# A two-layer convolution and feed-forward kernel: the even and odd tiles, the filter tiles and the squares of its start in another order

## The chip, the cores and the metric

The kernel runs on one core of a Trainium2 chip. Its time is the device time of one launch in microseconds (us). The kernel before the change took 943.13 us (median of three runs, 942.17 to 943.75).

Five engines of the core work side by side, each through its own list of instructions in order: TensorE (PE, matrix products; its weight loads are shown as PEld), VectorE (DVE), ScalarE (ACT), GpSimd (POOL) and SyncE (SP). PE writes to PSUM, from where DVE or ACT have to take ("evacuate") the result before the buffer can be written again. SP, POOL and ACT also issue the DMA transfers.

## The reference

Two kinds of layers alternate over a sequence of S = 2048 tokens with D = 576 channels, each twice: a gated long convolution A and a gated feed-forward B.

```python
def A(q, k, v, shift_k, ssm_k, ssm_D):
    kv = short_conv(k, shift_k) * v            # 4 taps per channel
    y  = irfft(rfft(kv, 2S) * rfft(ssm_k, 2S))[:S] + kv * ssm_D
    return q * y
def B(x):
    return (gelu(x @ w_gate) * (x @ w_up)) @ w_down     # 576 -> 4608 -> 576
x = A_q
x = x + A(layernorm(x)); x = x + B(layernorm(x))
x = x + A(layernorm(x)); x = x + B(layernorm(x))
```

The convolution y doesn't depend on x, so both A layers use the same y; only the gate q differs.

## The kernel before

**Tiling.** The sequence is cut into 4 blocks of 512 tokens (NB = 4, BS = 512). The convolution is a block convolution in the frequency domain: each block of kv and of the filter h is taken to 512 frequencies with a matrix product by a cosine and a sine matrix, the spectra are multiplied and summed over pairs of blocks, and an inverse product gives y of a block. A tile of frequencies (kt = 0 to 3) has 128 frequencies on the partitions and two parts s (cosine and sine) of 576 channels in the free dimension, which is cut in halves h of 288 (HW), one PSUM bank each. Filter tiles are made by `fwd_h` (line 182; 8 matmuls per part), kv tiles of block 0 by `fwd_full` (191; 8 matmuls per part). The matrices G (for h), F1 and F2 (for kv and the inverse) are made on the chip: angles, a mask on DVE (`mask`, 121), a sine on ACT (`sines`, 124).

Tokens lie four to a partition (i = 0 to 3). The frequencies of tile kt + 2 differ from those of tile kt by the sign of the odd i alone. `fwd_full` makes tiles 2 and 3 with a negated copy (`neg`) of the odd tokens. For the other blocks, `fwd_eo` (202) makes the sum of the even and that of the odd tokens in the two halves of a PSUM tile, 4 matmuls for each part and half of the channels; ACT copies both to an `eo` tile in float32, and `cross` (214) adds and subtracts them on DVE, which gives the tiles kt and kt + 2.

**Stages.** `Conv.begin` (476) writes the start of the kernel in a fixed order, engine by engine as the lines stand: matrices, kv of block 0, the filter tiles of all four blocks, y of block 0 (`inv0`), and then for each of the four 128-token groups j of block 0 a gate (`gate0`: two operations on DVE, then the mean on POOL, line 834, and the sum of squares on ACT, 842), its root on POOL (`root0`: 849, 850), the normalization on DVE (`norm0`, 1017), nine transposes on PE (`turn0`, 1028) and two copies on DVE (`copy0`, 1036). When all four groups are copied to xnT, the feed-forward matmuls (gu, line 1116) can begin. From there on a planner with a simple model of the engines' times (`Pace`) puts the convolution of the later blocks between the feed-forward matmuls. The change is in `begin` alone; the planner's order is the same after it.

**Buffers in the start.** `Conv.ps` (111) hands out PSUM tiles by turns, three from the pool that the transposes use too (3 buffers) and one from a pool with one buffer. Filter tiles of blocks 0, 2 and 3 go to buffers of the pools c_hr and c_kr and are stored to DRAM (Hd); those of block 1 stay in H1 and are stored too. Stores are not issued at once: `spill` (265) puts them in a list, and `flush` (271) issues what is in it on POOL; `h_tile` (571) and `kfwd` (612) flush what stood there before they add their own. The transposed filter blocks are loaded by `load_h` (493) on SP in two buffers, so that block 3's load waits until block 1's tiles have been made. Loads of weights (wgu, wd) are issued on SP too, k, v and x on POOL.

Of the kernel before, what the change touches and what calls it, by code (L numbers as in the profile page):

```python
# [14 lines left out]
BF16 = mybir.dt.bfloat16  # L15
# [3 lines left out]
P = 128  # L19
# [4 lines left out]
HW = 288  # L24
# [32 lines left out]
class Conv:  # L57
# [418 lines left out]
    def begin(self, gate0, root0, norm0, turn0, copy0, x0_stats, more, scratch, wide, stay):  # L476

        tc, nc, D = self.tc, self.nc, self.D
        with ExitStack() as es:
# [4 lines left out]
            ones = tmp.tile([1, P], BF16, name="ones")  # L484
# [8 lines left out]
            def load_h(b):  # L493
                t = hp.tile([P, RT, D], BF16, tag="h", name="h")
                nc.sync.dma_start_transpose(out=t[:], in_=self.hk[:, b * BS:(b + 1) * BS])
                return t
# [22 lines left out]
            G = tmp.tile([P, RT, 2 * NFQ], BF16, name="G")  # L519
# [2 lines left out]
            neg = scratch(BF16)  # L522
            jg = [ang[:, g * 4 * 2 * P:(g + 1) * 4 * 2 * P] for g in range(2)]
            jg.append(None)
            ps = self.ps()
            for _ in range(32):
                nc.tensor.matmul(ps[:, 0, 0:16], lhsT=ones[:], rhs=ones[:, 0:16], start=True, stop=True)

            def taps(j):
                ps = self.ps()  # L530
                for h in range(2):
                    nc.tensor.matmul(ps[:, h, 0:HW], lhsT=ones[:], rhs=sk1[:, h * HW:(h + 1) * HW, j], start=True, stop=True)
                nc.scalar.copy(out=self.halves(self.skc[:, j, :]), in_=ps[:, :, 0:HW])
# [8 lines left out]
                    taps(2)  # L542
            taps(1)
            taps(0)
            hT = {0: hp.tile([P, RT, D], BF16, tag="h", name="h")}
            for g in (1, 0):
                pt = self.psp.tile([P, 2, 1024], BF16, tag="pr", name="hps")
# [10 lines left out]
            flat = lambda F: F.rearrange("p i s j q -> p (i s j q)")  # L558

            def f_angles(g):  # L560
                if g == 2:
                    jg[2] = tmp.tile([P, 2, NFQ], I32, tag="dft_j", bufs=2, name="dft_j")[:].rearrange("p s f -> p (s f)")
                j4 = jg[g].rearrange("p (i s f) -> p i s f", i=2, s=2)
                cv = (colf[:] if g == 2 else col[:, 0:2, :]).rearrange("p t q -> p (t q)")
                for i in range(2):
                    row = 2 * i if g == 2 else 2 * g + i
                    for s in range(2):
                        nc.scalar.activation(out=j4[:, i, s, :], in_=cv, func=ACT.Identity, bias=offs[:, s:s + 1],
                                             scale=rowf[:, row:row + 1])

            def h_tile(b, kt, pool):
                if b == 1:
                    t = self.H1[:, kt, :, :]
                else:
                    t = pool.tile([P, 2, D], BF16, tag="kr" if pool is self.krp else "hr", name="h0")
                for s in range(2):
                    self.fwd_h(G, hT[b], kt, s, t)
                self.flush(0.0)
                self.spill(self.Hd[b][kt], t)
                return t  # L580
            h0 = {}
            self.H1 = stay()
            kv0 = deque(self.kv_ops(0))
# [3 lines left out]
            def negate(n):  # L587
                nc.scalar.mul(out=neg[:, n, :], in_=self.vt_[0][:, 2 * n + 1, :], mul=-1.0)
            for i in range(RT):
                h0[KTS[i]] = h_tile(0, KTS[i], self.hrp if i == 0 else self.krp)  # L590
                for _ in range(4):
                    kv0.popleft()[1]()
                if i == 1:
                    negate(0)
                if i < 2:
                    self.mask(jg[i])
                    self.sines(flat(Fs[i]), jg[i])
                if i < 1:
                    f_angles(i + 1)
                if i == 1:  # L600
                    more(0)
            hT[2] = load_h(2)
            h_tile(1, 0, self.hrp)
            more(1)
            h_tile(1, 2, self.hrp)
            self.load_k(1, nc.gpsimd)
            x0_stats(0)
            x0_stats(1)
            negate(1)
            kc, A = {}, {}  # L610

            def kfwd(kt):
                kc[kt] = self.kcp.tile([P, 2, D], BF16, tag="kc", name="kc")
                for s in range(2):
                    self.fwd_full(self.vt_[0], neg, kt, s, kc[kt])
                self.flush(0.0)
                self.spill(self.Kd[0][kt], kc[kt])

            def kacc(kt):
                for part in range(2):  # L620
                    t = self.ybp.tile([P, D], BF16, tag="yb", name="yb")
                    self.prod(part, kc[kt], h0[kt], t[:])
                    A[(part, kt)] = t
# [3 lines left out]
            def pair0(kt, sg):  # L627
                for part in range(2):
                    b = self.ybp.tile([P, D], BF16, tag="yb", name="yb")
                    nc.vector.tensor_tensor(out=b[:], in0=A[(part, kt)][:], in1=A[(part, kt + 2)][:],  # L630
                                            op=ALU.subtract if sg else ALU.add)
                    self.yb[(part, kt, sg)] = b

            def inv0(mt):
                self.inverse(0, mt, [(self.lhs(kt, s, mt, self.F2), self.yb[(s, kt, mt % 2)])
                                     for kt in range(2) for s in range(2)])
            kfwd(0)
            f_angles(2)
            kfwd(2)
            kacc(0)  # L640
            self.mask(jg[2])
            kfwd(1)
            kacc(2)
            self.sines(flat(self.F2[:]), jg[2])
            pair0(0, 0)
            kfwd(3)
            kacc(1)
            self.load_v(1, nc.gpsimd)
            kacc(3)
            pair0(1, 0)  # L650
            nc.scalar.activation(out=warm[:], in_=self.pis[:, 1:2], func=ACT.Gelu_apprx_tanh)
            h_tile(1, 1, self.hrp)
            h_tile(1, 3, self.hrp)
            hT[3] = load_h(3)
            h_tile(2, 0, self.hrp)
            h_tile(2, 2, self.krp)
            inv0(0)
# [9 lines left out]
            def kv1_ops(n):  # L667
                for _ in range(n):
                    next(ops)[1]()
            gate0(0)  # L670
            gate0(2)
            root0(0)
            gate0(1)
            h_tile(2, 1, self.hrp)
            root0(2)
            norm0(0)
            h_tile(2, 3, self.krp)
            gate0(3)
            root0(1)
            turn0(0)  # L680
            norm0(2)
            copy0(0)
            root0(3)
            norm0(1)
            h_tile(3, 0, self.hrp)
            turn0(2)
            copy0(2)
            norm0(3)
            turn0(1)
            copy0(1)  # L690
            turn0(3)
            kv1_ops(2)
            copy0(3)
            h_tile(3, 2, self.krp)
            kv1_ops(6)
            h_tile(3, 1, self.hrp)
            h_tile(3, 3, self.krp)
# [523 lines left out]
```

## Time and profile before

| | |
|---|---|
| time, median of three runs | 943.13 us |
| the profiled execution's own time | 943.32 us |
| its span | 941.5 us |
| PE busy | 926.9 us (98%) |
| DVE busy | 571.4 us (61%) |
| ACT busy | 295.9 us (31%) |
| POOL busy | 143.2 us (15%) |
| gu matmuls (L1116) | 565.5 us |
| first gu matmul, from the span's start | 62.71 us |

The busy times are sums over the whole span; a PE that is busy is not a PE at its peak. The profile's page gives the busy share in 40 slices of 23.5 us each, the first three of which hold the part of the kernel that the change touches. The chain of waits follows the work that ended last back from the last instruction, at each step to what released it. In the list of instructions in order of time, a line gives the start, the duration from the first start to the last end of the merged instructions, the engine, the line of the kernel, the operation, what is written from what, and how many instructions are merged; in brackets stands the idle time of the engine before it and what ended that. The lines of 2 us stretches give start and end, their length, then busy us (and instructions) of PE, PEld, DVE, ACT and POOL, the granted clock of PE, the busy share of the DMA engines and GB/s.

### The profile page before, as it was taken

Reading aid. Unit: us, or ns where it says so; the run is one execution under the profiler, and the core shown is the slowest. Engines: PE = TensorE matmul, PEld = TensorE weight load, DVE = VectorE, ACT = ScalarE, POOL = GpSimd, SP = SyncE. Lnnn points to the kernel's source line nnn. Section 1 sums busy time; section 2 is a strip of 40 time slices with the busy share of each in tenths; the row PEclk is TensorE's granted clock in tenths of the full one; section 3 lists DMA queues with packets and bytes.
Section 4 is the critical chain, followed back from the end, with each engine's and each line's share of the span. In section 5 each row is a group of like instructions: output and inputs, shape, how many; then the busy total and the mean of one; then the engine's idle time right before and its main releaser. Section 6 shows DMA issues by size and latency. Waiting matters only on the chain.

```text
span 941.5 us, 19061 instructions
## 1 busy us (share of the span) xinstructions
PE 926.9 (98%) x8128; PEld 536.5 (57%) x8128; DVE 571.4 (61%) x1027; ACT 295.9 (31%) x541; POOL 143.2 (15%) x303
## 2 busy tenths in 40 slices
PE   7989999999999999999999999999999999999998
PEld 5755564665655646546546556556556556556555
DVE  8977887898898637988982333663333335523332
ACT  8846214432124334231222421441221223311211
POOL 2453100511123104230100100230000002100000
PEclk9999999999999999999999999999999999999999
DMA  7989986765953522983930630891630630797720
GB/s 184 323 238 274 293 183 148 133 162 142 226 190 64 113 77 52 195 212 87 221 107 2 133 94 26 136 156 39 129 99 1 129 98 14 135 206 155 147 65 26
DMA packets 129065, 127.46 MB, mean 135 GB/s; under 512 B 45587, under 2 KB 121684, under 8 KB 128980
## 3 DMA queue, kind: packets, MB, share of 16 engines
q1 hardware_dynamic: 119904, 90.85, 45.7%
q0 software_dynamic: 8944, 34.49, 11.4%
q8 instruction: 63, 1.03, 0.5%
q10 hardware_dynamic: 132, 0.91, 0.4%
q14 instruction: 22, 0.18, 0.1%
HBM read 105.58 MB, written 10.62 MB: 123 GB/s over the span
## 4 chain that ended last, share of the span: by engine, by line
PE 91%; DMA 3%; DVE 2%; POOL 2%; ACT 1%; issue 1%; SPq 0%; POOLq 0%; DVEq 0%
PE gu L1116 59%; PE dn L1132 27%; DMA h<-in_A_ssm_k_dram 2%; PE cps L208 1%; PE cps L261 1%; PE ps L187 1%; DMA k<-in_A_k_dram 1%; POOL rstd L850 1%; PE ps L198 1%; DVE x_c L1161 0%; PE cps L187 0%; POOL ve L849 0%; ACT junk L842 0%; DVE x_c L877 0%; DMA xnT<-xn 0%
## 5 line engine op out<-in xcount | busy, mean ns | idle before, releaser
L1116 PE MATMUL gu<-xnT,wgu 64*128 64x512 bf16 x5184 | 565.5, 376 | 2.1 <-DVE x_c L1161 1.0
L1116 PEld LDWEIGHTS <-wgu 64*128 64x128 bf16 x5184 | 254.3, 94 | 305.2 <-issue 10.1
L1120 ACT ACTIVATE ga<-gu 128x512 f32<-128x512 f32 x288 | 171.9, 597 | 549.9 <-PE gu L1116 541.1
L1121 DVE TENSOR_TENSOR hT<-ga,gu 128x512 bf16<-128x512 f32 x288 | 197.6, 686 | 221.2 <-ACT ga L1120 219.7
L1132 PE MATMUL dn<-wd,hT 128*128 128x288 bf16 x2304 | 291.0, 286 | 0.5 <-DVE ob L1141 0.5
L1132 PEld LDWEIGHTS <-hT 128*128 128x128 bf16 x2304 | 223.5, 98 | 66.1 <-issue 10.5
L1166 DVE TENSOR_TENSOR x_c<-x_c,dn 128x576 f32<-128x576 f32 x64 | 48.2, 753 | 82.3 <-PE dn L1132 82.0
L834 POOL TENSOR_SCALAR nm<-s 128x1 f32<-128x1 f32 x60 | 21.1, 352 | 344.1 <-DVE x_c L1161 215.1
L842 ACT ACTIVATE junk<-x_c,nm 128x576 bf16<-128x576 f32 x48 | 37.0, 771 | 40.8 <-POOL nm L834 40.8
L327 POOL DMA_DIRECT2D hr<-Hd x32 | 17.3, 541 | 161.2 <-DVE prod L228 161.2
L850 POOL TENSOR_TENSOR rstd<-ve,neghalf_t 128x1 f32<-128x1 f32 x60 | 39.9, 665 | 5.0
L229 DVE TENSOR_TENSOR sum<-prod 128x576 bf16<-128x576 bf16 x72 | 33.0, 458 | 2.5
L187 PEld LDWEIGHTS <-G 128*128 128x128 bf16 x256 | 25.5, 100 | 11.2 <-issue 2.2
L187 PE MATMUL ps<-h,G 128*128 128x288 bf16 x192 | 27.6, 298 | 2.5 <-DMA h<-in_A_ssm_k_dram 1.7
L1152 DVE TENSOR_TENSOR ob<-x_c,dn 128x576 bf16<-128x576 f32 x15 | 11.2, 753 | 27.2 <-PE dn L1132 19.0
L163 DVE TENSOR_TENSOR kvt<-k,skc 128x1152 bf16<-128x1152 bf16 x32 | 23.9, 754 | 0.5
L849 POOL TENSOR_SCALAR ve<-ss 128x1 f32<-128x1 f32 x60 | 18.1, 301 | 32.4 <-ACT junk L842 32.3
L216 DVE TENSOR_TENSOR kc<-eo 128x288 bf16<-128x288 f32 x48 | 19.2, 453 | 2.1 <-ACT eo L211 2.1
L877 DVE SCALAR_TENSOR_TENSOR x_c<-g_t,rstd,x_c 128x576 f32<-128x576 f32 x16 | 13.1, 818 | 12.0 <-POOL rstd L850 11.9
L211 ACT COPY eo<-cps 128x576 f32<-128x576 f32 x24 | 15.3, 636 | 15.2 <-PE cps L208 12.7
L269 POOL DMA_DIRECT2D out_dram<-ob x12 | 6.7, 555 | 86.3 <-DVE ob L1152 86.2
L383 DVE TENSOR_TENSOR zs<-sum 128x576 f32<-128x576 bf16 x24 | 18.1, 755 | 0.5
(112 smaller groups left out, 464.7 us busy)
## 6 DMA issues: line engine op xcount, KB each, us to landing
wgu<-in_B_w_gate_dram SPq DMA_DIRECT2D x45, 576.0 KB, 5.7
wd<-in_B_w_down_dram SPq DMA_DIRECT2D x30, 864.0 KB, 6.7
wgu<-in_B_w_up_dram SPq DMA_DIRECT2D x45, 512.0 KB, 8.2
hr<-Hd POOLq DMA_DIRECT2D x32, 288.0 KB, 5.3
kr<-Kd POOLq DMA_DIRECT2D x24, 288.0 KB, 5.4
Hd<-h POOLq DMA_DIRECT2D x12, 288.0 KB, 4.6
Kd<-kc POOLq DMA_DIRECT2D x12, 288.0 KB, 6.6
k<-in_A_k_dram POOLq DMA_DIRECT2D x3, 1008.0 KB, 6.1
```

The source lines that it names most:

```text
L163: nc.vector.tensor_tensor(out=st[dst][:], in0=self.kt_[b][:, s0:s0 + 2, :], in1=self.skc[:, j, :].unsqueeze(1).to_broadcast([P, 2, D]), op ...
L187: nc.tensor.matmul(ps[:, h, 0:HW], lhsT=G[:, i, s * NFQ + kt * P: s * NFQ + (kt + 1) * P], rhs=src[:, i, h * HW:(h + 1) * HW], start=(n == ...
L216: self.nc.vector.tensor_tensor(out=dst, in0=eo[:, 0, :], in1=eo[:, 1, :], op=op)
L229: nc.vector.tensor_tensor(out=dst, in0=pr[:, 0, :], in1=pr[:, 1, :], op=ALU.subtract if part == 0 else ALU.add)
L834: nc.gpsimd.tensor_scalar(out=v["nm"][:], in0=v["s"][:], scalar1=-1.0 / D, scalar2=None, op0=ALU.mult)
L842: nc.scalar.activation(out=junk[:], in_=get_x(), func=ACT.Square, bias=v["nm"][:, 0:1], accum_out=v["ss"][:])
L850: nc.gpsimd.tensor_tensor(out=v["rstd"][:], in0=ve[:], in1=neghalf_t[:, 0:1], op=ALU.pow)
L1116: nc.tensor.matmul(pair[:, s, :], lhsT=w[r0:r0 + HK, k, gi * P:(gi + 1) * P], rhs=xnT[r0:r0 + HK, b, :], start=(k == 0), stop=(k == NKC - 1))
L1120: nc.scalar.activation(out=ga[:], in_=pair[:, 0, :], func=ACT.Gelu_apprx_tanh)
L1121: nc.vector.tensor_tensor(out=hT[:, fi, :], in0=ga[:], in1=pair[:, 1, :], op=ALU.mult)
L1132: nc.tensor.matmul(acc[:, h, 0:HW], lhsT=hT[:, fi, j * P:(j + 1) * P], rhs=wd[2 * wb + fi // WT][:, fi % WT, h * HW:(h + 1) * HW], start=( ...
L1166: nc.vector.tensor_tensor(out=xh, in0=xh, in1=acc[:, :, 0:HW], op=ALU.add)
```

## The change

Five things are changed in `begin`:

1. The tiles 0 and 2 of kv of block 0 are made by `fwd_eo` and `cross` as for the later blocks, in place of two calls of `kfwd` (two of `fwd_full` each). The statistics of x (`x0_stats`) stand after the matmuls, and their second half between the crosses.
2. The tiles (1,1) and (1,3) of the filter stand between the kv tiles 0/2, 1 and 3, and the load of the filter's block 3 behind (1,3). They stood behind all kv tiles.
3. The sines of F2 are issued behind the last kv tile's evacuations, and no longer ahead of them.
4. Filter tiles can be made in halves (one part s at a time, `h_half`). The tiles (2,1), (2,3), (3,0) and (3,2) are put in halves between the gates, roots, norms and transposes of block 0, so that the squares on ACT stand by turns with the evacuations of these halves.
5. Sixteen more of the small matmuls on `ones` (the kernel begins with 32 of them) stand ahead of the transposes of the first filter block.

```diff
+            warm_up(32)
...
             taps(0)
+            warm_up(16)
...
+            def h_half(b, kt, pool):
+                s = 1 if (b, kt) in half else 0
+                if s == 0:
+                    half[(b, kt)] = self.H1[:, kt, :, :] if b == 1 else pool.tile(
+                        [P, 2, D], BF16, tag="kr" if pool is self.krp else "hr", name="h0")
+                t = half[(b, kt)]
+                self.fwd_h(G, hT[b], kt, s, t)
+                if s == 1:
+                    self.flush(0.0)
+                    self.spill(self.Hd[b][kt], t)
+                return t
             def h_tile(b, kt, pool):
...
+                h_half(b, kt, pool)
+                return h_half(b, kt, pool)
...
             self.load_k(1, nc.gpsimd)
-            x0_stats(0)
-            x0_stats(1)
             negate(1)
...
-            kfwd(0)
+            for kt in (0, 2):
+                kc[kt] = self.kcp.tile([P, 2, D], BF16, tag="kc", name="kc")
+            eos = []
+            def eo0(s, h):
+                eos.append((s, slice(h * HW, (h + 1) * HW), self.fwd_eo(self.vt_[0], 0, s, h)))
+            def cross0():
+                s, cols, eo = eos.pop(0)
+                self.cross(eo, kc[0][:, s, cols], kc[2][:, s, cols])
+            for s in range(2):
+                for h in range(2):
+                    eo0(s, h)
+            x0_stats(0)
             f_angles(2)
-            kfwd(2)
+            for n in range(4):
+                cross0()
+                if n == 1:
+                    x0_stats(1)
+            self.flush(0.0)
+            for kt in (0, 2):
+                self.spill(self.Kd[0][kt], kc[kt])
             kacc(0)
+            h_tile(1, 1, self.hrp)
             self.mask(jg[2])
             kfwd(1)
             kacc(2)
-            self.sines(flat(self.F2[:]), jg[2])
+            h_tile(1, 3, self.hrp)
+            hT[3] = load_h(3)
             pair0(0, 0)
             kfwd(3)
+            self.sines(flat(self.F2[:]), jg[2])
             kacc(1)
...
             nc.scalar.activation(out=warm[:], in_=self.pis[:, 1:2], func=ACT.Gelu_apprx_tanh)
-            h_tile(1, 1, self.hrp)
-            h_tile(1, 3, self.hrp)
-            hT[3] = load_h(3)
             h_tile(2, 0, self.hrp)
...
             gate0(0)
+            h_half(2, 1, self.hrp)
             gate0(2)
+            h_half(2, 1, self.hrp)
             root0(0)
+            h_half(2, 3, self.krp)
             gate0(1)
-            h_tile(2, 1, self.hrp)
             root0(2)
             norm0(0)
-            h_tile(2, 3, self.krp)
+            h_half(2, 3, self.krp)
+            turn0(0)
+            h_half(3, 0, self.hrp)
             gate0(3)
             root0(1)
-            turn0(0)
             norm0(2)
             copy0(0)
             root0(3)
             norm0(1)
-            h_tile(3, 0, self.hrp)
+            h_half(3, 0, self.hrp)
             turn0(2)
             copy0(2)
             norm0(3)
+            h_half(3, 2, self.krp)
             turn0(1)
             copy0(1)
+            h_half(3, 2, self.krp)
             turn0(3)
             kv1_ops(2)
             copy0(3)
-            h_tile(3, 2, self.krp)
             kv1_ops(6)
```

## The prediction

> **What bounds the kernel now.** I read the page's 40 slices first (TensorE, PE, is full from the fourth slice on), then the chain of waits, then the first 63 us engine by engine, since every edit lies there: the first big matmul (gu, L1116) starts at 62.71 us. After it PE has no idle time up to 150 us, and 2.1 us in the 780 us from there on. So the change is worth what it moves that start, microsecond for microsecond.
>
> The chain of waits for these 63 us:
>
> ```profile
> 2.31 8.77 DMA k<-in_A_k_dram
> ...
> 21.18 2.12 PE ps L187 x16
> ...
> 37.05 15.08 DMA h<-in_A_ssm_k_dram
> ...
> 62.77 15.65 PE gu L1116 x144
> ```
>
> It names PE from 21 us and then the load of filter block 3. But a chain shows one of several tight paths. The busy time in stretches of 2 us (PE, PE's weight loads, VectorE = DVE, ScalarE = ACT, GpSimd = POOL) shows a second one:
>
> ```profile
> 26.00:28.00 2.00, 2.00 (x18) 1.61 (x17) 1.90 (x7) 1.79 (x4) 1.12 (x2) 1.00 0.96 249
> ...
> 36.00:38.00 2.00, 2.00 (x18) 1.52 (x16) 1.93 (x5) 1.99 (x6) 0.26 (x1) 1.00 1.05 408
> ...
> 42.00:44.00 2.00, 2.00 (x19) 1.60 (x17) 1.88 (x4) 1.30 (x2) 0.00 (x0) 1.00 1.09 341
> ```
>
> PE and DVE are both full: DVE's missing 0.03 to 0.12 us are the steps between instructions, and the view of waits names none for it from 24.65 to 48.2 us. The instructions in order of time show where they meet:
>
> ```profile
> 40.44 2.29 DVE L630 TENSOR_TENSOR yb<-yb 128x576 bf16<-128x576 bf16 x6
> 42.74 0.82 DVE L801 SCALAR_TENSOR_TENSOR x_c<-x_b,mv,y 128x576 f32<-128x576 bf16 x1
> ...
> 40.88 2.12 PE L261 MATMUL ps<-yb,F 128*128 128x288 bf16 x16
> ...
> 49.86 0.66 PE L1028 MATMUL xps<-ident,xn 128*128 128x128 bf16 x9 [0.98 <-ACT h L189]
> 52.17 2.13 PE L187 MATMUL ps<-h,G 128*128 128x288 bf16 x16 [1.65 <-DMA h<-in_A_ssm_k_dram]
> ...
> 56.22 0.68 PE L1028 MATMUL xps<-ident,xn 128*128 128x128 bf16 x9 [0.90 <-DVE xn L1017]
> ...
> 62.71 15.71 PE L1116 MATMUL gu<-xnT,wgu 64*128 64x512 bf16 x144
> ```
>
> PE enters the inverse (L261) at 40.88, just as DVE makes its inputs (L630); DVE enters the first gate (L801) at 42.74, just as the inverse is evacuated (42.06 + 0.65). After that PE has 3.5 us of holes, in brackets.
>
> **The change part by part.** Durations come from this execution; a 288-column matmul counts at its pitch, 0.98 us / 8 = 0.1225 us.
>
> The even and odd tiles. Two kfwd calls (2 x 2 x 8 = 32 matmuls) become four fwd_eo calls of 4: 16 fewer, 16 x 0.1225 = 1.96 us off PE. ACT still makes four evacuations (0.64 us each, L200 before, L211 later in this trace). DVE gains eight crosses: six of L216 later in the trace take 2.32 us, pitch (2.32 - 0.45) / 5 = 0.373, so 8 x 0.373 = 2.98 us, and nothing is taken off DVE. Their inputs come in time: the first eo copy ends near 27.05 (H1's last evacuation at 25.30, negate, copy, at 0.53 to 0.58 a step), DVE comes to it at 24.65 + 2 x 1.22 of statistics = 27.09. From 24.65 on DVE waited for nothing, so all that follows moves by 2.98: the second group of pair sums from 40.44 to 43.42, the first gate from 42.74 to 45.72.
>
> PE after the edit: four eo groups end at 25.10 + 1.96 = 27.06; tiles (1,1), kv 1, (1,3), kv 3, (2,0), (2,2) take 6 x 1.96 = 11.76, and 0.3 is lost where (1,3) waits for a PSUM buffer, because the four f_angles on ACT (2.07 us) now stand ahead of (1,1)'s evacuations: 39.2. Two of the four terms of inv0(0) take 0.49: 39.7. The third needs pair0(1,0), 43.42 + 0.45 = 43.9. PE stands still for 4.2 us: more than it was spared. The other 28 matmuls of the inverse, 3.43, with 0.25 for the fourth term, end at 47.5; (2,1) and (2,3) 3.92 later, at 51.45. Each evacuation of the inverse is done at least 0.3 us before its gate, so the gates keep DVE's time.
>
> Gates and the first transpose. Gates 0, 2 and 1 take 1.665 each (42.74, 44.41, 46.07): DVE is through at 50.7. norm0(0) needs POOL, whose order the edit alters: the store of tile (2,2), which stood behind rstd of gate 0, now stands ahead of it, since half tile (2,1) flushes it.
>
> ```profile
> 46.24 0.72 POOL L834 TENSOR_SCALAR nm<-s 128x1 f32<-128x1 f32 x1 [0.93 <-DVE x_c L806]
> 46.92 0.18 POOL L849 TENSOR_SCALAR ve<-ss 128x1 f32<-128x1 f32 x1
> 47.19 0.98 POOL L850 TENSOR_TENSOR rstd<-ve,neghalf_t 128x1 f32<-128x1 f32 x1
> ...
> 51.98 0.20 POOL L849 TENSOR_SCALAR ve<-ss 128x1 f32<-128x1 f32 x1
> 52.26 0.57 POOL L850 TENSOR_TENSOR rstd<-ve,neghalf_t 128x1 f32<-128x1 f32 x1
> ```
>
> ve would start at 46.92 + 2.98 + 0.54 to 0.62 (the issue) = 50.5; ve and rstd took 1.29 to the norm at 46.92, 0.88 at 51.98, so norm0(0) starts at 51.4 to 51.8, ends 0.70 later, and turn0(0) starts at 52.1 to 52.5. Before, it started at 49.86, held 0.98 by an evacuation queued behind three squares; the squares by turns remove that hold, but the transpose is later by more.
>
> The tail. From turn0(0) to gu the after kernel has four turns (0.52 each), and tiles (3,0) to (3,3) (1.96 each): 9.9 us. DVE's copies free the PSUM buffers of the halves of (3,2) about 0.2 us late, twice; with semaphores 0.5 in all. gu: 62.5 to 62.95. Before, the same work took 62.71 - 49.86 = 12.85: it held the 1.65 for block 3's filter and the 0.90, and a late turn now comes when PE has less left behind it, because half tiles stand between the gates.
>
> Moves at no cost. load_h(3) waits on SP for the last read of (1,3), 33.3 instead of 36.9; if it takes 15.1 as before it lands at 48.5, and its first reader comes at 52.6; cover 4 us, beyond that one for one. The third wgu load behind it on SP goes with it. load_v(1) on POOL waits for kv 3 to leave PE, 35.3 instead of 33.25; it lands some 9 us later, is read by L173 (63.04 before). The statistics' second half comes 1.5 us later and is used at 45.7. The last sines move on ACT from 32.64 to about 36, with the table load (1.28) behind them, so (2,0)'s evacuation ends at 39.05; inv0(0)'s buffer waits for that, and is covered by the wait for DVE. Halving the tiles adds no instruction. The 16 warm-up matmuls (32 took 1.02, so 0.5) stand at 5.6, where PE next waits for hn until 7.39; without that cover the 0.5 would reach DVE's copy at 9.78, and 0.05 of it the start of kv at 11.10, which waits for k.
>
> Sum on the profiled run's own time (943.32, span 941.5 plus 1.8; median shown 943.13): gu -0.2 to +0.25, so 943.1 to 943.6; I take the middle, **943.3**. On this kernel 0.2% (1.9 us, like the scatter 942.17 to 943.75) is what can be told from no change.
>
> **A rule against it.** PE's matmuls have two rates here, though the granted clock says 1.00 throughout:
>
> ```profile
> L187 PE MATMUL ps<-h,G x13: 396/444/448, 9.7 to 12.9; 128*128 128x288 bf16 x13
> ...
> L187 PE MATMUL cps<-h,G x7: 286/286/286, 13.7 to 14.5; 128*128 128x288 bf16 x7
> ```
>
> 444 ns while PE had just begun, 286 after some 6 us of work (7.39 to 13.3). From 48.9 to 52.2 PE did only 0.5 us of transposes and stayed at 286; a hole of 4.2 us is not in this trace. The Trainium skill, TensorE: Matmul & The Clock Gate, part 1, says that after an idle window of about 3.4 us the clock is halved, and that windows run freely; by it, as my estimate, such a hole would cool PE in about (4.2 - 3.4) / 3.4, a quarter, of the runs, with the sum of the second rival (945.0), and not otherwise. No stretch here shows which.
>
> **The rivals.**
> 1. PE is the bound after all, as the chain has it. Then 1.96 and the holes 0.98, 1.65 and 0.90 go: 5.5 us, 937.8. For it: PE is full from 21 to 48.9. Against: DVE's floor. Even with POOL at no time, norm0(0) ends at 50.7 + 0.7 = 51.4, and gu cannot start before 61.4 (942.0).
> 2. The hole of 4.2 us halves PE's rate (slower). Place: inverse and tile (2,1), from 43.9. At the 5.9 us that the start took to recover, half of it, 2.95, is lost: turn0(0) at 54.4, PE-bound from there, gu at 54.4 + 9.9 + 0.1 = 64.4, **945.0**; at 3.4 us cold 0.7, and with inverse tiles also late for gates 2 and 1 (0.4 to 0.6 each) up to 3: 944 to 946.5. It decides once PE's slack before turn0(0), 0.65 to 1.05, is used up. For: the 444 ns rows; against: the stretch from 48.9.
> 3. Block 3's filter, fetched while all DMA queues are full (share 1.0 to 1.3 from 38 to 50), lands after 52.6, or another wait in the tail: 945 to 946, only if the load takes over 19 us.
>
> **How the numbers follow.** Forecast 0.50; rival 1 0.12; rival 2 0.28, a good half beyond +0.2%; rival 3 and what I do not see 0.10. Faster 0.12; slower 0.16 + 0.10 = 0.26; same 0.50 + 0.12 = 0.62. The range leaves out rival 1 and the top of the others: 942.0, DVE's floor, to 946.0.
>
> **What would show it.** Right: pair0's group of six near 43.4, the first gate near 45.7, PE idle some 4 us inside inv0(0), turn0(0) near 52.3, no wait for block 3's filter, gu within 0.5 us of 62.7. Rival 2: matmuls of 444 ns behind the hole. Wrong: an inverse that does not wait for DVE, or DVE idle between 27 and 45 us.

## The result, and the profile after

The kernel after the change takes 945.01 us (median of 8 executions, 943.69 to 946.39) against 942.87 for the kernel before beside it (8 executions, 941.48 to 943.75): ratio 1.0025, 95% interval 1.0015 to 1.0036. Measured again unaltered in a later session (12 executions, below) it took 943.72 against 942.80: 1.0014, 1.0003 to 1.0026. So by the medians the change costs 0.9 to 2.1 us. That is at the edge of the 0.2% that was taken as the bound of what can be told; both intervals lie above 1. The forecast, 943.3, was 1.7 us under the first median and 0.4 under the second. The second rival, a hole that halves PE's rate, had 945.0.

The profiled execution of after took 944.92 us (span 943.2); its first big matmul starts at 64.58 us instead of 62.71. Own time less that start is 880.3 us, before 880.6; over the two kernels and all experiments it lies between 879.8 and 880.8. So all that follows is about the first 65 us.

The chain of waits of after between 9 and 66 us (start, us, engine, what, instructions):

```profile
26.79 0.65 ACT H L189
27.44 0.57 ACT ang L600
28.02 0.54 ACT eo L211
28.58 1.56 DVE kc L216 x4
...
45.07 0.38 DVE yb L640
45.49 0.77 PE ps L261 x4
46.27 1.57 PE cps L261 x8
47.83 3.04 PE ps L261 x16
...
54.80 0.50 PE xps L1061 x9
...
64.65 1.40 PE gu L1149 x11
```

Before, the chain ran over PE and then hung on block 3's filter load. Now it enters DVE with the first cross (L216) at 28.58, stays on DVE for 17 us, and goes to PE with the inverse (L261) at 45.49; from there PE has no more idle time up to gu. The filter load is gone from it.

The same in the instructions in order of time, DVE and then PE (idle time before, and what ended it, in brackets):

```profile
25.20 0.81 DVE L819 BATCH_NORM_STATS2 stats<-x_b 128x6 f32<-128x288 bf16 x2
...
28.58 1.56 DVE L216 TENSOR_TENSOR kc<-eo 128x288 bf16<-128x288 f32 x4 [0.85 <-ACT eo L211]
...
44.99 2.29 DVE L640 TENSOR_TENSOR yb<-yb 128x576 bf16<-128x576 bf16 x6
47.20 0.81 DVE L834 SCALAR_TENSOR_TENSOR x_c<-x_b,mv,y 128x576 f32<-128x576 bf16 x1
...
45.49 0.77 PE L261 MATMUL ps<-yb,F 128*128 128x288 bf16 x4 [4.24 <-DVE yb L640]
46.10 1.73 PE L261 MATMUL cps<-yb,F 128*128 128x288 bf16 x8
47.63 3.25 PE L261 MATMUL ps<-yb,F 128*128 128x288 bf16 x16
...
54.63 0.67 PE L1061 MATMUL xps<-ident,xn 128*128 128x128 bf16 x9
...
64.58 1.69 PE L1149 MATMUL gu<-xnT,wgu 64*128 64x512 bf16 x14
```

The second group of pair sums (L640, x6) moved from 40.44 to 44.99, the first gate (L834) from 42.74 to 47.20. PE stands still for 4.24 us inside the inverse. The 28 matmuls behind that hole take from 45.49 to 50.71, 5.2 us; at the pitch of 0.1225 they would take 3.43. The stretches of 2 us (after the length: PE, PEld, DVE, ACT, POOL, then the granted clock) say why:

```profile
42.00:44.00 2.00, 0.00 (x0) 0.00 (x0) 1.93 (x5) 0.18 (x1) 0.23 (x1) 1.00 1.03 406
...
46.00:48.00 2.00, 2.00 (x12) 1.37 (x11) 2.00 (x5) 0.78 (x2) 0.00 (x0) 0.63 1.03 362
48.00:50.00 2.00, 2.00 (x11) 1.26 (x10) 1.79 (x5) 0.73 (x2) 0.73 (x1) 0.52 1.14 234
50.00:52.00 2.00, 2.00 (x18) 1.60 (x17) 1.97 (x4) 1.53 (x3) 1.25 (x2) 1.00 1.19 237
```

From 42 to 44 us PE does nothing while DVE is full. From 46 to 50 the clock is granted at 0.63 and 0.52, and PE, busy all the time, starts 12 and 11 matmuls in a stretch that holds 18 in a warm one.

This execution has a second such place, earlier, which the next execution of the same kernel did not have:

```profile
19.05 4.77 PE L187 MATMUL ps<-h,G 128*128 128x288 bf16 x24 [2.01 <-ACT h L189]
```

PE stood for 2.01 us, the clock fell to 0.50 between 20 and 22, and 24 matmuls took 4.6 us instead of 2.94. PE thus reached the even and odd sums at 26.59 (before, kv's first tile at 25.10), and DVE had to wait 0.85 for the first copy, the bracket at 28.58.

### The profile page after: what moved, and what is told of

It is laid out like the page before. It is cut to its first block, busy times and chain, and to the rows that moved or that the text cites. A ratio compares the mean times of both kernels' runs of the same rounds, so it can differ in the third digit from the quotient of the medians.

```text
span 943.2 us, 19070 instructions
## 1 busy us (share of the span) xinstructions
PE 928.3 (98%) x8128; PEld 536.4 (57%) x8128; DVE 574.4 (61%) x1035; ACT 295.5 (31%) x541; POOL 140.6 (15%) x303
## 4 chain that ended last, share of the span: by engine, by line
PE 91%; DVE 4%; POOL 1%; DMA 1%; issue 1%; ACT 1%; SPq 0%; ACTq 0%; DVEq 0%
PE gu L1149 59%; PE dn L1165 27%; PE ps L187 2%; PE cps L261 1%; PE cps L208 1%; DMA k<-in_A_k_dram 1%; POOL rstd L883 1%; DVE x_c L1194 0%; PE cps L187 0%; PE ps L261 0%; DVE x_c L910 0%; DVE yb L229 0%; POOL ve L882 0%; DVE kc L216 0%; DVE prod L228 0%
## 5 line engine op out<-in xcount | busy, mean ns | idle before, releaser
L216 DVE TENSOR_TENSOR kc<-eo 128x288 bf16<-128x288 f32 x56 | 22.3, 453 | 3.0 <-ACT eo L211 3.0
L882 POOL TENSOR_SCALAR ve<-ss 128x1 f32<-128x1 f32 x60 | 17.3, 288 | 33.1 <-ACT junk L875 33.0
L261 PEld LDWEIGHTS <-F 128*128 128x128 bf16 x128 | 12.9, 104 | 10.2 <-issue 6.1
```

The costliest lines, as they stand in the source:

```text
L216: self.nc.vector.tensor_tensor(out=dst, in0=eo[:, 0, :], in1=eo[:, 1, :], op=op)
L261: nc.tensor.matmul(ps[:, h, 0:HW], lhsT=lhs, rhs=z[:, h * HW:(h + 1) * HW], start=(n == 0), stop=(n == len(terms) - 1))
```

## The experiments

The leading explanation after this result: the eight crosses push DVE's path back by 2.98 us, PE has to wait for it in a hole of over 4 us, and the hole cools PE, which costs up to 1.4 us more. Against it stood: that the 16 warm-up matmuls upset the start (the 2.01 us hole), that block 3's filter load is a floor of its own, and that the halved filter tiles and squares by turns (part 4) cost rather than save. Times are read at the first gate and at the start of gu in the profiled execution; the times are medians. The ratio, with its 95% interval, is estimated from the executions of the kernel and of the kernel before, run beside it, and can differ by up to 0.0011 from the quotient of the two medians.

### The even and odd tiles alone

The kernel before with part 1 alone; its statistics stay where they were.

```diff
-            kfwd(0)
...
+            for s in range(2):
+                for h in range(2):
+                    eos.append((s, slice(h * HW, (h + 1) * HW), self.fwd_eo(self.vt_[0], 0, s, h)))
             f_angles(2)
-            kfwd(2)
+            for s, cols, eo in eos:
+                self.cross(eo, kc[0][:, s, cols], kc[2][:, s, cols])
...
```

> The kernel before the change with nothing but the even and odd tiles (part 1 alone). Theory A (VectorE gains 2.98 us on a full path): first gate near 45.8, a hole of about 4 us in front of the inverse's third term with cold matmuls behind it, turn0(0) near 53, the first gu matmul near 65.5, time near 946, slower than with all five parts, since the old order has three squares ahead of an evacuation and three filter tiles behind the last transpose. Rival C (the new order from the gates on costs, the even and odd tiles gain): time under 943.

947.27 us, ratio 1.0035 (1.0022 to 1.0049); first gate at 47.39, gu at 66.20. In the profiled execution, in order of time:

```profile
38.12 2.08 PE L187 MATMUL cps<-h,G 128*128 128x288 bf16 x8 [3.99 <-ACT kc L200]
...
47.39 0.82 DVE L810 SCALAR_TENSOR_TENSOR x_c<-x_b,mv,y 128x576 f32<-128x576 bf16 x1 [0.90 <-ACT y L263]
```

Without the other parts the hole falls elsewhere: PE waits 3.99 us for an evacuation (L200) that stands on ACT behind the sine of F2, which waits for DVE's mask, and DVE is late with that. The clock fell to 0.50 between 38 and 40. So part 1 alone costs 2.7 us at gu (its distance from the first statistics on DVE is 40.75, before 38.06), slow matmuls behind the hole included. In after the distance is 39.38 and in after again, below, 37.91: parts 2 to 5 of the change win back 1.4 us in the one execution and all of it in the other.

### Part 4 undone

The kernel after, with the lines from gate0(0) on as they were before.

```diff
             gate0(0)
-            h_half(2, 1, self.hrp)
             gate0(2)
-            h_half(2, 1, self.hrp)
             root0(0)
-            h_half(2, 3, self.krp)
             gate0(1)
+            h_tile(2, 1, self.hrp)
...
+            h_tile(3, 2, self.krp)
```

> The kernel after the change with the order from the gates on (part 4: half tiles, squares by turns) put back to what it was. Theory A (part 4 helps by letting fewer tiles stand behind the late last transpose): turn0(0) near 54.7, the last transpose near 59.5, three filter tiles behind it, the first gu matmul at 65.5 to 66, time 946 to 947, about as the even and odd tiles alone (947.3). Rival C (part 4 costs): time under 944.5.

947.04 us, 1.0039 (1.0024 to 1.0054); first gate at 47.30, gu at 66.73.

```profile
55.03 0.66 PE L1057 MATMUL xps<-ident,xn 128*128 128x128 bf16 x9
...
60.18 0.74 PE L1057 MATMUL xps<-ident,xn 128*128 128x128 bf16 x9 [0.83 <-DVE xn L1046]
60.76 3.10 PE L187 MATMUL ps<-h,G 128*128 128x288 bf16 x24
...
66.73 1.47 PE L1145 MATMUL gu<-xnT,wgu 64*128 64x512 bf16 x12
```

From the first gate to gu it takes 19.43 us, with part 4 17.38: the halves and the order of the squares save 2.05 us. These are single executions: in the three others with part 4 and the hole (below) the distance is 16.84 to 17.99, so 1.4 to 2.6 us. Three tiles' worth of filter work are left behind the last transpose here, after waits that the halves fill. This is the gain that hides the crosses' cost in the total.

### The 16 warm-up matmuls taken out

```diff
             taps(0)
-            warm_up(16)
```

> The kernel after the change without the sixteen extra small matmuls. Theory A (they warm TensorE earlier, so that it runs ahead of ScalarE, stands still 2.0 us at 17 us and goes cold from 19.0 to 22.6): that hole falls back to about 0.7 us as before the change, no matmul of 444 ns between 19 and 23 us, the wait of VectorE for the eo copies (0.85) is gone, the first gate is near 46.3 instead of 47.2, the first gu matmul near 63.7 instead of 64.6, time about 944.1. Rival B (the hole came from k landing 0.46 us later in that execution): hole still 1.5 us or more, mean granted clock 0.996, time 945 as with them.

944.96 us, 1.0014 (1.0004 to 1.0024). The 2.01 us hole was gone and DVE did not wait for the first eo copy:

```profile
22.99 2.12 PE L187 MATMUL ps<-h,G 128*128 128x288 bf16 x16 [0.56 <-ACT h L189]
```

But that execution's filter rows landed 2 us late, PE waited 3.11 us for them at 9.31, and its statistics started at 26.46 instead of 25.20. The hole in the inverse was there as before (4.12 us), and gu came at 65.39. The time can't be told from after's: the warm-up matmuls are not the cause of the longer time. Whether they caused the 2.01 us hole of that one execution stays open, since this one's start was later too.

### The kernel's own full tiles back, the other parts kept

The kernel after without part 1's crosses; parts 2 to 5 stay.

```diff
...
-            for s in range(2):
-                for h in range(2):
-                    eo0(s, h)
+            kfwd(0)
             x0_stats(0)
             f_angles(2)
-            for n in range(4):
-                cross0()
-                if n == 1:
-                    x0_stats(1)
...
+            kfwd(2)
+            x0_stats(1)
```

> The kernel after the change with block 0's kv tiles 0 and 2 made by kfwd as before (parts 2 to 5 of the change kept). Theory A (VectorE is the second bound and the eight crosses are what costs): the first gate goes back to 42.7 to 43.4, the inverse does not wait for VectorE (hole under 0.5 us, no cold matmuls there), turn0(0) near 50.5, the first gu matmul at 60.5 to 61.5, time 941 to 942, faster than before the change. Rival C (the new order from the gates on, with the store ahead of the root and the halves between, is what costs): the first gu matmul stays above 63.5, time 944 or more.

950.19 us, 1.0061 (1.0041 to 1.0082): the slowest of all, where 941 to 942 had been expected. DVE did what it was to do, the rest did not:

```profile
43.36 0.82 DVE L817 SCALAR_TENSOR_TENSOR x_c<-x_b,mv,y 128x576 f32<-128x576 bf16 x1 [0.25 <-ACT y L263]
...
49.73 0.68 PE L1044 MATMUL xps<-ident,xn 128*128 128x128 bf16 x9 [0.52 <-DVE xn L1033]
54.92 2.10 PE L187 MATMUL ps<-h,G 128*128 128x288 bf16 x8 [4.51 <-DMA h<-in_A_ssm_k_dram]
...
66.50 1.69 PE L1132 MATMUL gu<-xnT,wgu 64*128 64x512 bf16 x14
```

The gate is back at 43.36, no hole is left in the inverse, and the first transpose starts at 49.73. Then tile (3,0) waits 4.51 us for block 3's filter, and the clock is 0.62, 0.50, 0.50 and 0.67 in the stretches from 52 to 60. So the filter is a floor of its own. Its load on SP, and the time from issue to landing in the answer on DMA issues:

```profile
35.47 12.23 SPq L495 DMA_TRANSPOSE h<-in_A_ssm_k_dram  x1
...
h<-in_A_ssm_k_dram SPq DMA_TRANSPOSE x1, 19.4
```

It is issued at 35.47 and lands at 54.9. In after it takes 17.3 us (34.86 to 52.16), in before 15.1 (37.05 to 52.13). Six weight loads (wgu) stand on SP ahead of it in all three; over the eight profiles with these six loads ahead it was issued between 33.56 and 41.80 and landed between 50.4 and 54.9. The wait of 4.51 explains the profiled execution, which was the best of six. The three executions with a mean granted clock of 0.996 took 946.35 to 949.58, the three with 0.994 took 950.80 to 953.08: the longest ones were also the ones that lost most clock. What made them so no profile shows.

### The hole filled

The kernel after, with 30 idle matmuls into a PSUM tile of their own ahead of the third term of inv0(0).

```diff
...
+        fill = self.ps() if filler else None
         for n, (lhs, z) in enumerate(terms):
+            if filler and n == 2:
+                for _ in range(filler):
+                    nc.tensor.matmul(fill[:, 0, 0:HW], lhsT=self.ident[:], rhs=self.skc[:, 0, 0:HW], start=True, stop=True)
...
```

> The kernel after the change with 30 matmuls of 288 columns into an unused PSUM tile behind the second term of the first inverse tile, 3.7 us in the hole of 4.2 us. Theory A (the hole halves TensorE's rate afterwards): the inverse's 28 matmuls at 286 ns throughout, turn0(0) bound by VectorE at about 54.05 instead of 54.63, the first gu matmul 0.2 to 0.6 us earlier, time 944.4 to 944.8. Rival D (the slow rate has another cause than the idle time, or the rate does not matter): matmuls of 444 ns still behind 45.5 us, or the start of gu unchanged at 64.6.

944.57 us, 1.0005 (0.9995 to 1.0015). The clock was 1.00 throughout, and the inverse had its pitch back. (The fill also takes one turn of the PSUM buffers, so that the tiles behind it sit in other buffers than in after.) In order of time:

```profile
44.07 3.71 PE L265 MATMUL ps<-yb,F 128*128 128x288 bf16 x28 [0.39 <-DVE yb L644]
...
54.22 1.14 PE L187 MATMUL cps<-h,G 128*128 128x288 bf16 x8 [1.40 <-DMA h<-in_A_ssm_k_dram]
```

What the fill gained went into the next floor: the filter, issued at 33.56, took 20.6 us, and PE waited 1.40 for it. Hence the next three.

### Filter block 3 ahead of two weight loads: with the hole filled, with the hole, and before

One edit on three kernels: the filled one (f1), after (h1) and before (g1). `more(1)` issues the weight loads wgu 0 and 1, six transfers.

```diff
             h_tile(1, 0, self.hrp)
-            more(1)
...
             hT[3] = load_h(3)
+            more(1)
```

> The kernel after the change with the 30 fill matmuls of the run before, and with the load of filter block 3 ahead of the first two weight loads (wgu 0 and 1) on SP instead of behind them. Theory E (block 3's filter lands at 52 to 55 us whenever it is issued, because it shares the DMA queues with 2.3 MB of weights, and that is a third floor under the tail): it lands before 48 us, the 1.40 us wait of tile (3,0) is gone, the first gu matmul 0.5 to 1.2 us earlier than in the run with the fill alone (63.66), ratio to the kernel before below 1.0005. Rival F (its landing is set by the transposing load itself): it lands 14 us or more after its issue, no gain.

> The kernel after the change with the load of filter block 3 ahead of wgu 0 and 1, and no fill matmuls. Against the run that has both, it differs in the fill alone, with no wait for the filter in either. Theory A (the hole of 4.2 us in the first inverse tile halves TensorE's rate behind it): granted clock about 0.5 to 0.6 from 45 to 50 us, matmuls of 444 ns, the first gu matmul 0.6 to 2 us later than with the fill (61.7), ratio to before 1.001 to 1.003. Rival D (the hole is harmless): same time as with the fill, ratio 1.0005 or less.

> The kernel before the change with nothing but the load of filter block 3 ahead of wgu 0 and 1. Theory E: it lands before 49 us, the wait of 1.65 us at 52 us is gone, the first gu matmul 0.9 to 1.7 us earlier (61.0 to 61.8), time 0.8 to 1.6 us below the kernel before in the same job. Rival F: it lands near 52 as before, same time.

| kernel | median, before beside it | ratio | first gate | gu | gate to gu |
|---|---|---|---|---|---|
| f1, filled | 942.98, 942.29 | 1.0005 (0.9992 to 1.0017) | 45.06 | 61.69 | 16.63 |
| h1, with the hole | 944.28, 942.80 | 1.0013 (1.0003 to 1.0023) | 47.00 | 64.99 | 17.99 |
| g1, before with the load ahead | 941.54, 942.29 | 0.9984 (0.9972 to 0.9996) | 42.41 | 61.22 | 18.81 |

The load lands 10.8 to 11.6 us after its issue in all three, and nobody waits for it. Between f1 and h1 only the 30 matmuls in the hole differ, with their PSUM tile. The inverse in f1 (by line: shortest, median and longest ns), and a stretch of h1:

```profile
L265 PE MATMUL ps<-yb,F x28: 283/286/287, 43.4 to 46.8; 128*128 128x288 bf16 x28
```

```profile
46.00:48.00 2.00, 2.00 (x11) 1.22 (x9) 1.84 (x5) 0.65 (x1) 0.00 (x0) 0.50 1.06 295
48.00:50.00 2.00, 2.00 (x10) 1.30 (x9) 1.73 (x4) 0.65 (x1) 0.24 (x1) 0.50 1.13 220
```

In h1 the 28 matmuls took 6.0 us (45.16 to 51.13) instead of 3.5, and gu came 1.36 us later behind its gate than in f1. The ratios alone don't separate the two, since their intervals overlap and they ran in different sessions. In before (g1) the load's place is worth 0.75 us by the medians and 0.4 to 2.6 us by the interval of the ratio: its wait of 1.65 is gone.

### After again, unaltered

> The kernel after the change, unaltered, for the comparison within one job. Both theories: ratio to before 1.0015 to 1.0036 as measured. Theory E: its block 3 filter lands at 52 to 55 us again, and in some executions after tile (3,0) is ready for it.

943.72 us, 1.0014 (1.0003 to 1.0026); gu at 62.86. DVE and PE in order of time:

```profile
27.39 1.56 DVE L216 TENSOR_TENSOR kc<-eo 128x288 bf16<-128x288 f32 x4
...
46.02 0.82 DVE L834 SCALAR_TENSOR_TENSOR x_c<-x_b,mv,y 128x576 f32<-128x576 bf16 x1
...
44.18 1.12 PE L261 MATMUL ps<-yb,F 128*128 128x288 bf16 x4 [4.12 <-DVE yb L640]
...
52.81 0.67 PE L1061 MATMUL xps<-ident,xn 128*128 128x128 bf16 x9
...
62.86 1.47 PE L1149 MATMUL gu<-xnT,wgu 64*128 64x512 bf16 x12
```

No wait for eo here, but the same hole, and the 28 matmuls take 4.7 us (44.18 to 48.89). PE stood 1.65 us at 17 instead of 2.01, and the clock stayed 1.00 there.

The mean granted clock of every execution, profiled or not, tells how often PE was cooled:

| kernels | executions by mean granted clock |
|---|---|
| after, after again, h1, e1 (hole of 4.1 to 4.2 us) | 20 at 0.996, 24 at 0.998 |
| e3, f1 (the same, hole filled) | 20 at 1.00, 3 at 0.999, 1 at 0.998 |
| before, beside these | 69 at 1.00, 4 at 0.999, 8 at 0.998, 1 at 0.996 |

The four kernels whose profiles show the hole lost clock in all 44 executions; with the hole filled, 23 of 24 lost next to nothing, so the loss comes with the hole, and the start ahead of it seldom costs any. In the profiles the time at half clock, worked out from the shares in the stretches (twice the missing share times 2 us), comes in two sizes: 3.4 us (after again, e4, f4, and twice in after, once behind the early hole) and 6.8 us (h1, e1, e2). Half a clock over 3.4 us is 0.0018 of 942 us, so 0.998 is one such phase and 0.996 two, or a long one. Within each of the four kernels the executions at 0.996 were the longer ones (by 0.45, 0.75, 0.68 and 1.77 us, 0.96 on the weighted mean; when the clocks are shuffled within the kernels so large a mean comes in about 1 of 1,000). So 3.4 us more of half clock, 1.7 us of PE's work, goes with 0.96 us of the total. That the clock alone makes this difference is not shown: a late start, for one, could lengthen both.

### A version that beats both

f2 is the kernel with the full tiles back and the load of block 3 ahead; h3 is f2 without the 16 warm-up matmuls as well.

```diff
             h_tile(1, 0, self.hrp)
-            more(1)
...
+            kfwd(0)
...
+            kfwd(2)
...
             hT[3] = load_h(3)
+            more(1)
```

```diff
             taps(0)
-            warm_up(16)
```

> The kernel after the change with kv tiles 0 and 2 made by kfwd as before, and with the load of filter block 3 ahead of wgu 0 and 1. Theory E plus A (without the crosses VectorE is early, and what made the run with kfwd slow was tile (3,0) standing 4.5 us for block 3's filter and TensorE cold behind that): no wait for the filter, no cold matmuls behind 25 us, turn0(0) near 49.7, the first gu matmul at 60 to 61, time 940.5 to 942, scatter back to 2 or 3 us, faster than before the change. Rival C (the new order from the gates on costs by itself): the first gu matmul above 63, time above 944.

> The fastest kernel so far (kfwd for tiles 0 and 2, block 3's filter ahead of wgu 0 and 1) without the sixteen extra small matmuls. Theory A' (they move TensorE's early work by up to 1 us and nothing that VectorE or the tail waits for): same time within 0.1%, ratio to before 0.996 to 0.998. Rival B' (the warm-up earns something): ratio 0.998 or more.

f2: 939.65 us, 0.9968 (0.9956 to 0.9981), faster than both kernels. h3: 940.65, 0.9980 (0.9970 to 0.9991), not told apart from f2. In f2:

```profile
43.28 0.82 DVE L817 SCALAR_TENSOR_TENSOR x_c<-x_b,mv,y 128x576 f32<-128x576 bf16 x1 [0.26 <-ACT y L263]
...
49.64 0.68 PE L1044 MATMUL xps<-ident,xn 128*128 128x128 bf16 x9 [0.51 <-DVE xn L1033]
50.16 1.14 PE L187 MATMUL ps<-h,G 128*128 128x288 bf16 x8
...
59.95 1.25 PE L1132 MATMUL gu<-xnT,wgu 64*128 64x512 bf16 x10
```

```profile
h<-in_A_ssm_k_dram SPq DMA_TRANSPOSE x1, 8.2
```

The filter lands 8.2 us after its issue instead of 19.4, the next tile follows the transpose at once, and gu starts 6.55 us earlier than in the kernel that differs from it by the order of the loads alone.

f2 also prices part 1 with nothing else in the way, since nobody waits for the filter in it, in f1 or in h1. From f2 to f1 part 1 and the fill are added: gu comes 2.68 us later behind the first statistics (35.00, 37.68), and the time is 3.33 us longer in the same session (939.65, 942.98; the intervals of the ratios lie apart). From f2 to h1 part 1 alone is added: 4.18 us at gu (39.18), and ratios of 0.9968 and 1.0013, which is 4.2 us. So the crosses cost some 2.7 to 3.3 us, and with the hole that they open about 4.2.

## Why the prediction was right, and where it was wrong

**DVE is a second full path: right.** The crosses were to push the gate by 2.98. From the first statistics to the first gate DVE took 18.09 us before and 21.07 in after again: 2.98. In the first execution of after it took 22.00; 0.85 of the rest is the wait for eo. With the full tiles back (e2, f2) it took 18.34 and 18.33, 0.25 of it a wait for the inverse's evacuation.

**"The first eo copy ends near 27.05", DVE comes to it at 27.09: too tight to be a step.** It held in after again (first cross at 27.39, no wait) and failed in after (28.58, 0.85 of wait), where PE had been cooled before (0.50 from 20 to 22 us). A cover of 0.04 us should have been given a price in the range.

**The start of DVE's path.** The forecast took 24.65 from before's execution; over the runs it lay between 24.01 and 26.46, with the loads at the start. The three kernels whose start is that of before had 24.32 to 25.45, so at least part of this scatter has nothing to do with the change; it is 0.55 of after's 1.87 us at gu.

**PE stands still for 4.2 us: right** (4.24 and 4.12). **What it costs: the step that failed.** The forecast put the other 28 matmuls at 3.43 us and the cooling into a rival with a chance of 0.28. They took 4.7 to 6.0 us, and 44 of 44 executions lost clock. The first transpose was therefore set by PE in both profiled executions of after, not by DVE and POOL: at 54.63 and 52.81, each 3.92 us behind the end of the inverse (50.71 and 48.89). The first line is after's norm, the other two are f1's norm and first transpose:

```profile
53.28 0.58 DVE L1050 TENSOR_SCALAR xn<-x_c,nm,rstd 128x576 bf16<-128x576 f32 x1 [1.08 <-POOL rstd L883]
...
50.78 0.58 DVE L1054 TENSOR_SCALAR xn<-x_c,nm,rstd 128x576 bf16<-128x576 f32 x1 [0.73 <-POOL rstd L887]
51.42 0.68 PE L1065 MATMUL xps<-ident,xn 128*128 128x128 bf16 x9 [0.44 <-DVE xn L1054]
```

In f1 PE waits for the norm and starts 0.64 us behind its start; in after it starts 1.35 behind it and in after again 0.90 (norm at 51.91), so PE was late by 0.71 and 0.26. The norm itself comes 0.36 and 0.17 later behind the first gate than in f1 (6.08, 5.89 and 5.72): in after the first square (ACT, 51.46) stands behind the inverse's last evacuation (50.91), which the slow matmuls made late. The gates of after kept DVE's time, as forecast; in after again the second gate came 0.12 late (47.81), just behind its evacuation (47.13 + 0.65), so the forecast cover of 0.3 us was gone there. The size of the whole at gu: from gate to gu 16.63 us without cooling (f1), 16.84, 17.38, 17.85 and 17.99 with it (after again, after, e1, h1), so 0.2 to 1.4 us. The rival's own 1.7 us lies above all four, and its time of 945.0 was met in the first session with the help of the late start and the wait for eo. That both medians lie inside 942.0 to 946.0 is owed, for the first of them, to the upper end, which was set for the rivals; the 943.3 itself left out a cost that came every time. In after again, where that cost was 0.2 us, gu came at 62.86, inside the forecast's 62.5 to 62.95.

The Trainium skill, TensorE: Matmul & The Clock Gate, part 1, has the clock halved after at least one idle window of about 3.4 us, with windows that run freely. The trace agrees that the moment wanders: by the shares in the stretches the clock fell some 2 us after the hole began in e1 (0.91 from 42 to 44 us, the hole from 41.58) and some 5 in after (0.63 from 46 to 48, the hole from 41.25). It does not agree that the idle time has to hold a whole such window: a hole of 2.01 us cooled PE. My estimate from that section, a quarter of the runs, was far off: it was all of them.

**The tail: right.** 9.9 to 10.4 us from the first transpose to gu were forecast; 9.95 and 10.05 came. Part 4 earns some 2 us, and no transpose is held by a square.

**"It lands at 48.5 ... cover 4 us": wrong, without consequence in after.** It was issued at 34.86, not 33.3, took 17.3 us, not 15.1, and landed at 52.16. Its reader came at 55.13, because PE was late; in the filled kernel, where PE was not, it waited 1.40. So the third rival's floor lies just behind the first two: 19 us of loading were called the condition, and 19.4 and 20.6 were seen.

**Rival 1 (PE the bound, 937.8): refuted.** 16 fewer matmuls on PE only made it wait.

**The warm-up matmuls and the moves at no cost.** No time is told apart with or without the 16. Parts 2 and 3 were never run alone; that they cost nothing is not shown by itself, only that parts 2 to 5 together gain (f2 against g1, both with the load ahead: 939.65 and 941.54 in the same session, gu at 59.95 and 61.22).

Left open: how much of the 0.9 to 2.1 us is cooling in the medians (the profiles say 0.2 to 1.4), what parts 2 and 3 are worth each, why the full tiles with the loads in after's order scatter up to 953 us, and what sets the scatter of the first loads.

## What to carry to other kernels

Where two engines are both full, work moved from one to the other can cost its whole duration, as the 2.98 us of crosses did here, however little it looks in the sums over the span; find the second path before spending on the first. A hole that opens in TensorE in the middle of a dense phase is to be priced with the slow matmuls behind it, or filled with idle work (1.36 us at gu here by the profiles, not told apart in the total). And when one path is shortened, look at what the loads do next: here the same kernel went from 950.19 to 939.65 us by the order of one transposed load and six weight loads on a queue.

## What the runs showed of the hardware

- A hole of 2.01 us halved the granted clock once (0.50 between 20 and 22 us in after); one of 1.65 at the same place did not. Holes of 3.99 to 4.51 us did it in every profile that had one.
- The clock can fall after the work has come back: in after the hole ended at 45.49 and the stretch from 44 to 46 was still granted 1.00, the next 0.63.
- The time at half clock, by the shares in the stretches, was 3.4 us in five phases and 6.8 us in three, never in between.
- The same transposed load of a filter block takes 12.4 to 20.6 us behind six weight loads on its queue and 8.1 to 11.6 ahead of them. In e2 and f2 it occupies SP's issue for 12.23 and 2.57 us.
